# Reading two kinds of PSUM bank at the scheduler's high priority, in a kernel of windowed attention and a feed-forward layer

## The chip, the cores and the metric

The kernel runs on one core of a Trainium2 chip. The metric is the device time of one execution in microseconds (us). Three runs of the kernel before took 719.66, 725.25 and 728.06 us; the median is 725.25 us. One further execution was recorded by the hardware profiler; all views come from it.

Names of engines: PE is TensorE (matmuls), PEld its loading of weights, DVE is VectorE, ACT ScalarE, POOL GpSimd, SP SyncE, whose queue issues most DMAs.

## The reference: what is computed

Attention over q, k, v of shape 4 x 8 x 768 x 64 (batch, heads, positions, head size), where a position sees the last 128 positions and the first 4 ("sinks"), followed by a feed-forward layer on 3072 rows of 512 with a piecewise quadratic activation:

```python
scores = scale * np.matmul(q, k.transpose(0, 1, 3, 2))
keep = is_sink | in_window
a = np.exp(scores - max); a = a / (a.sum() + 1e-9)
x = (a @ v)                      # heads side by side: 3072 x 512
h = x @ w_in                     # 512 -> 2048
g = np.where(h >= 1, h, np.where(h <= -1, 0.0, (h + 1) ** 2 / 4))
out = g @ w_out                  # 2048 -> 512
```

## The kernel before

**Units and waves.** A unit is one batch, one head and half of the positions (3 tiles of 128 rows): 64 units. Eight units, one for each head, make a wave; the attention of a wave runs beside the feed-forward layer of the wave before, so TensorE always has matmuls of both. The first 16 units (the first two waves) take another way, in pairs (`pair_scores`, `early_transp`, `pair_av`). The other 48 are "split" units: each float32 operand is split into a rounded high part and a low remainder, and products are made of the parts. These 48 are what the change touches.

**One split unit, by lines.** `load` brings q and k and splits them (L222 and L225 on ScalarE, L224 on VectorE, L226 on GpSimd). `scores` makes three banks of scores, one for each tile (L240); VectorE reads a bank with the mask and the row maximum (L244), ScalarE takes the exponential (L247), and after the third tile GpSimd and VectorE normalise p (L252, L253, L256, L259) and copy the columns of the sinks to `sk` (L261). `transp`, a unit later, transposes the three tiles of p and `sk` into one bank (L295, L296). That bank is read four times: by ScalarE into the high part of the tiles (L298), by VectorE into their low part (L299), by ScalarE into the high part of the sinks (L300) and by VectorE into their low part (L301). GpSimd then masks the tiles (L304 and L306, each twice) and spreads the sinks (L308). `av`, another unit later, multiplies with v into one bank (L342), which ScalarE (L343) and VectorE (L344, L345) read into the layer's input `xn`. v is split in `values` (L272, L277 on ScalarE, L273, L278 on GpSimd). Tile "r" has one buffer, in which q and v of successive units take turns.

**The feed-forward layer.** `stage1` makes a bank of h (L489); ScalarE and VectorE apply the activation and split the result (L496, L497 on ScalarE, L498 on VectorE, L499 on ScalarE, L500 on VectorE), `stage2` multiplies with the second weights (L508). In 32 units of the later waves `recheck` loads a tile of weights again and takes its top bytes (L196 on ScalarE); in every second of them VectorE folds two such tiles into `both` (L198); L595 to L598 evaluate `both` once, in the last of these.

**What sets the order.** TensorE's order is written out by hand (`attn_steps`, `moe_steps` and `spread`; the pool is entered with `manual_schedule` for TensorE alone). For the other engines the framework's scheduler decides: it plays the program in modelled time and gives an engine, of what is ready, the instruction with the highest priority, which without more is the one that stands first in the program. What it so orders is then fixed: on the chip each engine runs its instructions in that order, and a waiting instruction holds all behind it.

**The banks.** Scores, transposes and p times v share a pool of three banks, `ps_a` (L57). TensorE uses five per unit, in the order scores, scores, scores, transposes, p times v. With three banks that means: the first scores of a unit wait for the last L244 of the unit before, the second scores for L299 and L301 (the bank of transposes), the third for L345 (the bank of p times v), the transposes for the first L244, and p times v for the second L244. Where L345 stands ahead of L301, the second and third scores change places.

Of the kernel before, what the change touches and what calls it, by code (L numbers as in the profile page):

```python
# [8 lines left out]
F32 = mybir.dt.float32  # L9
# [4 lines left out]
ALU = mybir.AluOpType  # L14

B, H, S, D = 4, 8, 768, 64
DM, DFF = 512, 2048
P = 128
# [31 lines left out]
def attn_ffn(ctx, tc, qk, qkp, vx, vs, par, w_in, w_out, out):  # L50
    nc = tc.nc
# [68 lines left out]
    for r0 in (0, 32):  # L120
        r = r0 + CT * NSINK
# [5 lines left out]
    sk1 = const.tile([44, P], F32R, name="sk1")  # L127
# [154 lines left out]
    def transp(u):  # L282
        b, h, t0 = u
        p, sk = st.pop(("p", u))
        T = CT * P
        i0 = int(t0 == 0)
        ns = CT - i0
        r = ns * NSINK
        spt = st["sp", u] = sp[units.index(u) % 2]
        ps = ps_a.tile([P, 512], F32, name="ps_a")  # L290
        pk = ps[:r, T:512]
        pt = st["pt", u] = att.tile([P, 2, CT, 2, P], F32R, name="pt")
        pth, ptl = pt[:, 0], pt[:, 1]
        for i in range(CT):
            nc.tensor.transpose(ps[:, i * P:(i + 1) * P], p[:, i, KB:260], ident)  # L295
        nc.tensor.transpose(pk, sk, ident)  # L296
        full = ps[:, :T].rearrange("p (i q) -> p i q", q=P)
        nc.scalar.copy(pth[:, :, 1], full)  # L298
        nc.vector.tensor_tensor(ptl[:, :, 1], full, pth[:, :, 1].bitcast(F32), op=ALU.subtract)  # L299
        nc.scalar.copy(sk1[0:r], pk)  # L300
        nc.vector.tensor_tensor(sk1[32:32 + r], pk, sk1[0:r].bitcast(F32), op=ALU.subtract)  # L301
        for t in (pth, ptl):
            src = t[:, i0:, 1].bitcast(F32)
            nc.gpsimd.affine_select(out=t[:, i0:, 0], in_=src, pattern=[[0, ns], [-1, P]], base=-1,  # L304
                                    channel_multiplier=1, compare_op=ALU.is_ge, fill=0.0)
            nc.gpsimd.affine_select(out=t[:, i0:, 1], in_=src, pattern=[[0, ns], [1, P]], base=0,  # L306
                                    channel_multiplier=-1, compare_op=ALU.is_ge, fill=0.0)
        nc.gpsimd.tensor_tensor(spt[0:44].rearrange("r (t q) -> r t q", q=P)[:, :ns],  # L308
                                sk1.bitcast(F32).unsqueeze(1).broadcast_to([44, ns, P]),
                                tsel[:, :ns].unsqueeze(2).broadcast_to([44, ns, P]), op=ALU.mult)  # L310

    def av(u):
        b, h, t0 = u
        T = CT * P
        i0 = int(t0 == 0)
        ns = CT - i0
        pt = st.pop(("pt", u))
        spt = st.pop(("sp", u))
        v_s, vs_s = st.pop(("v", u))
        ps = ps_a.tile([P, 512], F32, name="ps_a")  # L320
        r0 = (h % 2) * D
        x = xn[r0:r0 + D, h // 2, :]

        terms = [(2 * CT - 1, 2 * CT)] + [(2 * i + 1, 2 * i + 3) for i in range(CT - 1)] + [None]
        if t0:
            terms.append((0, 1))
        mms = []
        for n, t in enumerate(terms):  # L330
            if t is None:
                w, rhs, c = vs_s, [spt[:, :ns * P]], i0
            else:
                s0, s1 = t
                w, c = v_s[:, (s0 + 1) // 2 - i0], s0 // 2
                rhs = [pt[:, j].rearrange("p i c q -> p (i c q)")[:, s0 * P:s1 * P] for j in range(2)]
                if n == 0:
                    rhs = [pt[:, :, CT - 1, 1]]
            mms += [(w.rearrange("p a d -> p (a d)"), y, c * P) for y in rhs]
        for n, (w, y, c) in enumerate(mms):  # L340
            z = ps[:, c:c + (2 * P if len(y.shape) == 3 else y.shape[-1])]
            nc.tensor.matmul(z, lhsT=w, rhs=y, start=(n == 0), stop=(n == len(mms) - 1))  # L342
        nc.scalar.copy(x, ps[D - r0:P - r0, :T])  # L343
        nc.vector.tensor_tensor(x, ps[r0:r0 + D, :T], x, op=ALU.add)  # L344
        nc.vector.tensor_tensor(x[:, T - P:], ps[r0:r0 + D, T:512], x[:, T - P:], op=ALU.add)  # L345


    def pair_load(m):
# [117 lines left out]
    def attn_steps(n):  # L466
        us = {k: units[n - k] for k in (-1, 0, 1, 2) if 0 <= n - k < len(units)}
        steps = []
        if n == NATIVE:
            steps.append((0.0, lambda: load(us[0])))  # L470
        if -1 in us:
            steps.append((0.0, lambda: load(us[-1])))
        if 1 in us and n - 1 >= NATIVE:
            steps.append((0.0, lambda: values(us[1])))
        steps += [(0.22, lambda i=i: scores(us[0], i)) for i in range(CT) if 0 in us]
        steps += [(0.43, lambda: transp(us[1]))] if 1 in us and n - 1 >= NATIVE else []
        steps += [(1.0, lambda: av(us[2]))] if 2 in us and n - 2 >= NATIVE else []
        if n in CHECK:
            steps.append((0.0, lambda: recheck(n - CHECK[0], n)))
        return steps  # L480
# [119 lines left out]
    ps = ps_a.tile([P, 512], F32, name="ps_a")  # L600
# [56 lines left out]
    with tc.If(other_v > 0):  # L657
        with tc.tile_pool(name="gen", bufs=1) as gen:
# [9 lines left out]
            for t0 in (0, CT):  # L668
                keep = gen.tile([P, CT, S], F32, name="keep")
                kidx = gen.tile([P, S], I32, name="kidx")  # L670
                r = gen.tile([P, S], F32, name="r")
# [55 lines left out]
```

## Time and profile before

| | |
|---|---|
| three runs | 719.66, 725.25, 728.06 us |
| the profiled execution | 724.25 us, of which 722.5 us from first to last instruction |
| mean granted clock of TensorE | 0.991 |
| TensorE busy | 691.1 us, 96% |
| VectorE, ScalarE, GpSimd busy | 530.1, 496.4 and 304.7 us |
| DMA | 73.04 MB, 101 GB/s on average |

The split units run from about 120 to 635 us; after 636 us only the feed-forward layer of the last wave is left. How to read the rows that follow: a row of the timeline has start, length, engine, line, operation, output<-input and, in brackets, the idle time of the engine before it and what ended that. A row of waits has the waiting engine and line, the line waited for, and us in total, times, longest.

Where the text speaks of X, Y and Z, these are three neighbouring units. They recur in each of three waves, those that run near 340, 427 and 514 us, and their instructions stand there in nearly the same order. X is the unit whose rows begin near 427 us in the middle one, Y near 438, Z near 448.

### The profile page before, as it was taken

To read this page: it belongs to the slowest core of one execution; us is meant where nothing else is said; L and a number is where in the kernel's file an instruction comes from. 1 tells how busy PE (TensorE), PEld (TensorE's weight loads), DVE (VectorE), ACT (ScalarE), POOL (GpSimd) and SP (SyncE) were. 2 spreads that over 40 slices of the span, in tenths; PEclk is the share of its full clock that TensorE was granted. 3 is DMA by queue.
4 is the path that set the end of the run, shared out by engine and by line. 5 is a ranking of instruction groups with operands and counts; after the bars stand their busy time and mean duration, and the time that the engine had idled before them with its cause. 6 is when DMAs were issued, how large, how long until landed. Compare 5 with 4: busy or idle time off the path is not lost.

```text
span 722.5 us, 12238 instructions
## 1 busy us (share of the span) xinstructions
PE 691.1 (96%) x3873; PEld 609.8 (84%) x3873; DVE 530.1 (73%) x1345; ACT 496.4 (69%) x1289; POOL 304.7 (42%) x514
## 2 busy tenths in 40 slices
PE   5689999899999999999999999999989999999996
PEld 3467777799899999899889987999979999989895
DVE  8888898978776878788778788878887687733221
ACT  5776777686687877787777777778766867544432
POOL 2003334754452555365555556646556364400000
PEclk9899999999999999999999999999999999999999
DMA  7844333332243434244333443334412220001001
GB/s 230 296 169 166 131 125 96 111 100 57 55 136 97 130 117 124 72 159 126 107 94 86 149 126 115 115 105 140 126 46 69 79 69 17 8 1 44 1 0 49
DMA packets 44840, 73.04 MB, mean 101 GB/s; under 512 B 13024, under 2 KB 29408, under 8 KB 44768
## 3 DMA queue, kind: packets, MB, share of 16 engines
q1 hardware_dynamic: 41504, 59.59, 27.3%
q10 hardware_dynamic: 3264, 12.58, 4.8%
q8 instruction: 33, 0.54, 0.3%
q14 instruction: 39, 0.32, 0.1%
HBM read 65.87 MB, written 6.29 MB: 100 GB/s over the span
## 4 chain that ended last, share of the span: by engine, by line
PE 73%; DVE 15%; ACT 6%; DMA 2%; issue 2%; POOL 1%; SPq 0%; ACTq 0%; DVEq 0%; POOLq 0%
PE o_ps L508 30%; PE h_ps L489 29%; PE ps_a L342 4%; PE ps_a L240 4%; PE ps_a L295 2%; DVE k_s L224 2%; DVE p L259 1%; DVE bits L153 1%; PE ps_a L432 1%; DVE g L498 1%; DMA w<-w_in 1%; DVE gl L500 1%; ACT p L247 1%; DVE p L256 1%; DMA r<-qk 1%
## 5 line engine op out<-in xcount | busy, mean ns | idle before, releaser
L489 PE MATMUL h_ps<-x,wi 128*128 128x384 f32 x1536 | 310.0, 341 | 1.0 <-DVE g L498 1.0
L489 PEld LDWEIGHTS h_ps<-x,wi 128*128 128x128 f32 x1536 | 263.6, 189 | 11.5 <-issue 1.5
L508 PE MATMUL o_ps<-w,gh 128*128 128x512 f32 x768 | 244.4, 399 | 0.0
L508 PE MATMUL o_ps<-w,gl 128*128 128x512 f32 x384 | 151.3, 394 | 0.0
L508 PEld LDWEIGHTS o_ps<-w,gh 128*128 128x128 f32 x768 | 134.3, 189 | 17.7 <-issue 2.8
L496 ACT ACTIVATE g<-h_ps,half 128x384 f32<-128x384 f32 x128 | 73.9, 577 | 59.1 <-PE h_ps L489 58.0
L498 DVE SCALAR_TENSOR_TENSOR g<-g,h_ps 128x384 f32<-128x384 f32 x128 | 70.2, 548 | 57.4 <-ACT g L497 56.4
L226 POOL TENSOR_TENSOR q_l<-r,q_h 128x384 fp32r<-128x384 f32 x48 | 50.4, 1049 | 135.7 <-ACT q_h L225 109.1
L499 ACT CAST gh<-g 128x384 fp32r<-128x384 f32 x128 | 65.5, 512 | 57.6 <-DVE g L498 57.0
L508 PEld LDWEIGHTS o_ps<-w,gl 128*128 128x128 f32 x384 | 72.2, 188 | 17.8
L500 DVE TENSOR_TENSOR gl<-g,gh 128x384 fp32r<-128x384 f32 x112 | 69.0, 616 | 24.4 <-ACT gh L499 23.5
L247 ACT ACTIVATE p<-p,peak 128x260 f32<-128x260 f32 (+1 forms) x144 | 71.4, 496 | 15.8 <-DVE peak L244 15.1
L224 DVE TENSOR_TENSOR k_s<-k_r,k_s 64x524 fp32r<-64x524 f32 (+1 forms) x44 | 47.1, 1070 | 43.3 <-ACT k_s L222 43.2
L244 DVE CUSTOM_DVE_ANT_0 p<-ps_a,m 128x260 f32<-128x260 f32 (+1 forms) x144 | 57.2, 408 | 17.5 <-PE ps_a L240 16.6
L497 ACT ACTIVATE g<-g 128x384 f32<-128x384 f32 x128 | 67.0, 523 | 2.6
L306 POOL TENSOR_SCALAR_AFFINE_SELECT pt<-pt 128x384 fp32r<-128x384 f32 (+1 forms) x96 | 51.3, 534 | 24.0 <-DVE pt L299 21.0
L304 POOL TENSOR_SCALAR_AFFINE_SELECT pt<-pt 128x384 fp32r<-128x384 f32 (+1 forms) x96 | 51.8, 539 | 7.4 <-ACT pt L298 3.1
L259 DVE TENSOR_SCALAR p<-p,stat 128x132 f32<-128x132 f32 (+1 forms) x144 | 54.4, 431 | 0.1
L500 POOL TENSOR_TENSOR gl<-g,gh 128x384 fp32r<-128x384 f32 x16 | 21.9, 1370 | 68.4 <-ACT gh L499 60.5
L342 PEld LDWEIGHTS ps_a<-pt,v_s 128*128 128x128 f32 x304 | 46.4, 188 | 2.2
L342 PE MATMUL ps_a<-pt,v_s 128*128 128x256 f32 (+1 forms) x304 | 46.7, 273 | 0.0
L240 PE MATMUL ps_a<-k_s,q_h 128*128 128x260 f32 (+1 forms) x144 | 40.5, 281 | 5.1 <-DVE sk L301 3.9
(149 smaller groups left out, 1007.7 us busy)
## 6 DMA issues: line engine op xcount, KB each, us to landing
r<-qk SPq DMA_DIRECT2D x48, 192.0 KB
k_r<-qk SPq DMA_DIRECT2D x32, 262.0 KB
again<-w_in SPq DMA_DIRECT2D x16, 512.0 KB
again<-w_out SPq DMA_DIRECT2D x16, 512.0 KB
w<-w_in ACTq DMA_DIRECT2D x6, 1024.0 KB
w<-w_out ACTq DMA_DIRECT2D x6, 1024.0 KB
out<-o SPq DMA_DIRECT2D x23, 256.0 KB
r<-vx SPq DMA_DIRECT2D x32, 128.0 KB
```

Source lines behind the costliest of these rows:

```text
L224: eng.tensor_tensor(k_s[D:P], k_r[D:P], k_s[D:P].bitcast(F32), op=ALU.subtract)
L240: nc.tensor.matmul(ps[:, lo:260], lhsT=q[:, i * P:(i + 1) * P], rhs=k_s[:, c0:c0 + 260 - lo], start=(j == 0), stop=(j == len(qs) - 1))
L247: nc.scalar.activation(p[:, i, lo:260], p[:, i, lo:260], AF.Exp, bias=peak_i, scale=-1.0, accum_out=stat[:, i:i + 1])
L259: nc.vector.tensor_scalar(p[:, i, lo:260], p[:, i, lo:260], stat[:, CT + i:CT + i + 1], None, op0=ALU.mult)
L342: nc.tensor.matmul(z, lhsT=w, rhs=y, start=(n == 0), stop=(n == len(mms) - 1))
L489: nc.tensor.matmul(h_ps[:, :T], lhsT=w_i[j][:, w, ct * P:(ct + 1) * P], rhs=x[:, y, ct], start=(ct == 0 and n == 0), stop=(ct == NCT - 1 a ...
L496: nc.scalar.activation(g, h_ps[:, :T], AF.Relu, bias=half, scale=0.5)
L497: nc.scalar.activation(g, g, AF.Square)
L498: nc.vector.scalar_tensor_tensor(g, g, 1.0, h_ps[:, :T], op0=ALU.min, op1=ALU.max)
L499: nc.scalar.copy(gh, g)
L500: (nc.gpsimd if row0 == GL_POOL else nc.vector).tensor_tensor(gl, g, gh.bitcast(F32), op=ALU.subtract)
L508: nc.tensor.matmul(o_ps[tt], lhsT=gg[:, tt * P:(tt + 1) * P], rhs=w_o[j][:, w], start=(j == 0 and n == 0), stop=(j == NJ - 1 and n == 2))
```

## The change

The four instructions that read a bank of transposes, and the three that read a bank of p times v, are recorded under the scheduler's high priority. Among the first four, the two for the sinks now stand ahead of the two for the tiles.

```diff
-        nc.scalar.copy(pth[:, :, 1], full)
-        nc.vector.tensor_tensor(ptl[:, :, 1], full, pth[:, :, 1].bitcast(F32), op=ALU.subtract)
-        nc.scalar.copy(sk1[0:r], pk)
-        nc.vector.tensor_tensor(sk1[32:32 + r], pk, sk1[0:r].bitcast(F32), op=ALU.subtract)
+
+        with tc.high_priority():
+            nc.scalar.copy(sk1[0:r], pk)
+            nc.scalar.copy(pth[:, :, 1], full)
+            nc.vector.tensor_tensor(sk1[32:32 + r], pk, sk1[0:r].bitcast(F32), op=ALU.subtract)
+            nc.vector.tensor_tensor(ptl[:, :, 1], full, pth[:, :, 1].bitcast(F32), op=ALU.subtract)
...
-        nc.scalar.copy(x, ps[D - r0:P - r0, :T])
-        nc.vector.tensor_tensor(x, ps[r0:r0 + D, :T], x, op=ALU.add)
-        nc.vector.tensor_tensor(x[:, T - P:], ps[r0:r0 + D, T:512], x[:, T - P:], op=ALU.add)
+        with tc.high_priority():
+            nc.scalar.copy(x, ps[D - r0:P - r0, :T])
+            nc.vector.tensor_tensor(x, ps[r0:r0 + D, :T], x, op=ALU.add)
+            nc.vector.tensor_tensor(x[:, T - P:], ps[r0:r0 + D, T:512], x[:, T - P:], op=ALU.add)
```

No instruction is added, dropped or resized, and TensorE's order is the same. In the changed kernel line numbers shift: L300 and L301 (high parts, sinks then tiles), L302 and L303 (low parts) are what were L300, L298, L301 and L299; the masks L304 and L306 become L306 and L308, the sinks' spreading L308 becomes L310, L344 and L345 become L347 and L348, L498 and L500 become L501 and L503. The text names lines by their numbers before, unless it says otherwise.

VectorE in unit X of the wave near 427 us, before (p is the probabilities, pt the transposed ones, sk_133 the sinks' parts, xn the layer's input, g and gl the activation and its low part; ISA with ps_a is the reading of a bank of scores, L244):

```order
L299 TENSOR_TENSOR pt<-ps_a,pt 128x3x128
L259 TENSOR_SCALAR p<-p,stat 128x132 x3
L261 COPY sk<-p 128x12
L344 TENSOR_TENSOR xn<-ps_a,xn 64x384
L301 TENSOR_TENSOR sk_133<-ps_a,sk_133 12x128
L345 TENSOR_TENSOR xn<-ps_a,xn 64x128
L498 SCALAR_TENSOR_TENSOR g<-g,h_ps 128x384
L244 ISA p,peak<-ps_a,m_106 128x260
L244 ISA peak 128x1
L500 TENSOR_TENSOR gl<-g,gh 128x384
L244 ISA p,peak<-ps_a,m_106 128x260
```

The same place in the changed kernel:

```order
L302 TENSOR_TENSOR sk_133<-ps_a,sk_133 12x128
L303 TENSOR_TENSOR pt<-ps_a,pt 128x3x128
L259 TENSOR_SCALAR p<-p,stat 128x132 x3
L261 COPY sk<-p 128x12
L347 TENSOR_TENSOR xn<-ps_a,xn 64x384
L348 TENSOR_TENSOR xn<-ps_a,xn 64x128
L501 SCALAR_TENSOR_TENSOR g<-g,h_ps 128x384
L503 TENSOR_TENSOR gl<-g,gh 128x384
L244 ISA p,peak<-ps_a,m_106 128x260
L244 ISA peak 128x1
L244 ISA p,peak<-ps_a,m_106 128x260
```

The sinks' low part now stands ahead of the tiles'; in this unit, and in X of the two other waves, gl has moved ahead of the first reading of scores as well.

VectorE in unit Y, which follows, before:

```order
L500 TENSOR_TENSOR gl<-g,gh 128x384
L299 TENSOR_TENSOR pt<-ps_a,pt 128x3x128
L259 TENSOR_SCALAR p<-p,stat 128x132 x3
L198 TENSOR_TENSOR both<-both,top 128x256
L261 COPY sk<-p 128x12
L344 TENSOR_TENSOR xn<-ps_a,xn 64x384
L301 TENSOR_TENSOR sk_133<-ps_a,sk_133 12x128
L345 TENSOR_TENSOR xn<-ps_a,xn 64x128
L498 SCALAR_TENSOR_TENSOR g<-g,h_ps 128x384
L500 TENSOR_TENSOR gl<-g,gh 128x384
```

And in the changed kernel:

```order
L302 TENSOR_TENSOR sk_133<-ps_a,sk_133 12x128
L303 TENSOR_TENSOR pt<-ps_a,pt 128x3x128
L259 TENSOR_SCALAR p<-p,stat 128x132 x2
L503 TENSOR_TENSOR gl<-g,gh 128x384
L259 TENSOR_SCALAR p<-p,stat 128x132
L198 TENSOR_TENSOR both<-both,top 128x256
L347 TENSOR_TENSOR xn<-ps_a,xn 64x384
L261 COPY sk<-p 128x12
L348 TENSOR_TENSOR xn<-ps_a,xn 64x128
L501 SCALAR_TENSOR_TENSOR g<-g,h_ps 128x384
```

The sinks' low part has moved six places up, and the first gl from ahead of the tiles' low part to between two of the three normalisations. The second part of xn keeps its place.

GpSimd in unit Y, before (stat is the sum of p, sp_136 the spread sinks, vsx and v_s the low parts of v):

```order
L252 TENSOR_SCALAR stat<-stat 128x3
L304 AFFINE_SELECT pt<-pt 128x3x128
L306 AFFINE_SELECT pt<-pt 128x3x128
L304 AFFINE_SELECT pt<-pt 128x3x128
L278 TENSOR_TENSOR vsx_137<-vs_r,vsx_137 44x64
L273 TENSOR_TENSOR v_s<-r,v_s 128x4x64
L306 AFFINE_SELECT pt<-pt 128x3x128
L308 TENSOR_TENSOR sp_136<-sk_133,tsel 44x384
```

And in the changed kernel:

```order
L252 TENSOR_SCALAR stat<-stat 128x3
L306 AFFINE_SELECT pt<-pt 128x3x128
L310 TENSOR_TENSOR sp_136<-sk_133,tsel 44x384
L308 AFFINE_SELECT pt<-pt 128x3x128
L306 AFFINE_SELECT pt<-pt 128x3x128
L278 TENSOR_TENSOR vsx_137<-vs_r,vsx_137 44x64
L273 TENSOR_TENSOR v_s<-r,v_s 128x4x64
L308 AFFINE_SELECT pt<-pt 128x3x128
```

The spreading of the sinks has moved from the end of the unit's row to its second place among the masks.

Besides these, three output stores move ahead of one load of the sinks' v on SyncE, once in each of three waves, and L596, one of the instructions that evaluate `both`, moves behind L498 in Y of the wave near 514 us.

## The prediction, made before the result was known

> **What bounds the kernel now.** I read the page's busy times first.
>
> ```profile
> span 722.5 us, 12238 instructions
> ...
> PE 691.1 (96%) x3873; PEld 609.8 (84%) x3873; DVE 530.1 (73%) x1345; ACT 496.4 (69%) x1289; POOL 304.7 (42%) x514
> ```
>
> TensorE is busy for 691.1 of 722.5 us. The change touches split units only, so I then took the busy time by stretches, four of them from the part with split units. The columns are start:end, length, and busy us (instructions) of PE, PEld, DVE, ACT and POOL, then clock, DMA share and GB/s.
>
> ```profile
> 216.00:300.00 84.00, 84.00 (x477) 76.66 (x476) 64.85 (x180) 64.94 (x171) 42.12 (x81) 1.00 0.38 116
> 340.00:385.00 45.00, 43.88 (x247) 39.32 (x246) 36.29 (x95) 31.99 (x83) 26.98 (x47) 1.00 0.37 109
> 427.00:470.00 43.00, 40.92 (x234) 36.89 (x233) 35.58 (x94) 31.93 (x83) 26.32 (x46) 1.00 0.38 113
> 514.00:555.00 41.00, 38.93 (x224) 34.97 (x223) 33.79 (x91) 29.03 (x79) 24.59 (x40) 1.00 0.27 74
> ```
>
> From 216 to 300 TensorE has no gap at all: nothing that VectorE or ScalarE does sooner can help there. The other three stretches have 1.12, 2.08 and 2.07 us of gaps, 5.3 us together. The list of TensorE's waits says for what (total us, times, longest):
>
> ```profile
> PE ps_a L240 <- DVE sk L301: 3.9, 5, 1.4
> ...
> PE ps_a L295 <- DVE p L259: 2.3, 1, 2.3
> ...
> PE ps_a L240 <- DVE xn L345: 0.8, 2, 0.4
> ...
> PE ps_a L295 <- DVE peak L244: 0.6, 1, 0.6
> ```
>
> 3.9 us are a scores matmul waiting for a bank of transposes that L301 (the sinks' low part) reads last, 0.8 us one waiting for a bank of p times v (L345), 0.6 us a transpose waiting for a bank of scores (L244). The sum is those 5.3 us. The 2.3 us for L259 are one wait of the first transposes for p itself, before any bank has been read by the lines of the change; no moved instruction feeds it. Here is the largest gap, in unit Y of the wave that begins near 427 us, and its neighbours X (before) and Z (after); start and length in us:
>
> ```profile
> 430.43 0.36 PE L240 MATMUL ps_a<-k_s,q_h 128*128 128x260 f32 x1 [0.28 <-DVE sk L301]
> ...
> 432.38 0.49 PE L295 MATMUL ps_a<-ident,p 128*128 128x128 f32 x3
> ...
> 439.43 0.69 PE L489 MATMUL h_ps<-x,wi 128*128 128x384 f32 x3
> 441.54 0.36 PE L240 MATMUL ps_a<-k_s,q_h 128*128 128x260 f32 x1 [1.42 <-DVE sk L301]
> ...
> 442.89 0.28 PE L240 MATMUL ps_a<-k_s,q_h 128*128 128x260 f32 x1
> ...
> 443.83 0.49 PE L295 MATMUL ps_a<-ident,p 128*128 128x128 f32 x3
> ...
> 451.61 0.36 PE L240 MATMUL ps_a<-k_s,q_h 128*128 128x260 f32 x1 [0.39 <-DVE xn L345]
> ```
>
> The end of a matmul normally lies under the next one. The page's group of L489 has the mean of one:
>
> ```profile
> L489 PE MATMUL h_ps<-x,wi 128*128 128x384 f32 x1536 | 310.0, 341 | 1.0 <-DVE g L498 1.0
> ```
>
> One lasts 0.34 us, three together 0.69 (at 439.43), so they start some 0.17 apart and the last 0.16 or so of each is hidden. A gap then costs its idle time and about 0.16 more: the scores of 441.54 could have begun at 439.43 + 0.53 = 439.96. Eight gaps: 5.3 + 8 x 0.16 = 6.6 us is all that the change can win, 0.9%.
>
> VectorE over X and Y:
>
> ```profile
> 430.32 0.29 DVE L345 TENSOR_TENSOR xn<-ps_a,xn 64x128 f32<-64x128 f32 x1
> 430.64 0.56 DVE L498 SCALAR_TENSOR_TENSOR g<-g,h_ps 128x384 f32<-128x384 f32 x1
> 431.12 0.42 DVE L244 CUSTOM_DVE_ANT_0 p<-ps_a,m 128x260 f32<-128x260 f32 x1
> ...
> 431.78 0.56 DVE L500 TENSOR_TENSOR gl<-g,gh 128x384 fp32r<-128x384 f32 x1 [0.23 <-ACT gh L499]
> 432.25 0.42 DVE L244 CUSTOM_DVE_ANT_0 p<-ps_a,m 128x260 f32<-128x260 f32 x1
> ...
> 434.74 1.09 DVE L224 TENSOR_TENSOR k_s<-k_r,k_s 64x524 fp32r<-64x524 f32 x1 [0.88 <-ACT k_s L222]
> ...
> 437.13 0.54 DVE L299 TENSOR_TENSOR pt<-ps_a,pt 128x384 fp32r<-128x384 f32 x1
> 437.60 1.28 DVE L259 TENSOR_SCALAR p<-p,stat 128x132 f32<-128x132 f32 x3
> 438.80 1.74 DVE L198 TENSOR_TENSOR both<-both,top 128x256 int32<-128x256 int32 x1
> ...
> 441.11 0.28 DVE L301 TENSOR_TENSOR sk<-ps_a,sk 12x128 fp32r<-12x128 f32 x1
> 441.42 0.28 DVE L345 TENSOR_TENSOR xn<-ps_a,xn 64x128 f32<-64x128 f32 x1
> ...
> 442.75 0.56 DVE L500 TENSOR_TENSOR gl<-g,gh 128x384 fp32r<-128x384 f32 x1 [0.58 <-ACT gh L499]
> 443.22 0.42 DVE L244 CUSTOM_DVE_ANT_0 p<-ps_a,m 128x260 f32<-128x260 f32 x1
> ```
>
> L301 ends at 441.39, and TensorE goes on at 441.54. But L345, due for the next scores' bank, ends at 441.70, and L244, due for the transposes' bank, at 443.64. These two stand right behind.
>
> **The change part by part.** *L301 ahead of L299* (L300 ahead of L298 on ScalarE): the transposes' bank is free when L299 ends. In Y that would be 437.67 + 0.31 for the L301 before it, 438.0, against a wish for 439.96: the wait on L301 goes, by 2 us. Nothing is added; the same 0.28 us stand earlier, so the sum up to L345 is the same. L299 and what hangs on it (the masks on GpSimd, p times v a unit later) come 0.3 us later; p times v of that unit stands a whole unit further on in TensorE's order, and the list of waits has none of L342.
>
> *What is late next, if nothing else moved.* Without the wait TensorE wants the next scores at 439.96 + 1.35 (442.89 - 441.54) = 441.3, L345 gives the bank at 441.7; it then wants the transposes 0.94 later at 442.65 and gets the bank at 443.64 + 0.05. The transposes start at 443.7 instead of 443.83. Of 1.58 us freed, 0.1 stays. The rest turns into waits on L345 and L244, which end a row of steps through ScalarE (L498, L499, L500, L244) that the change doesn't shorten.
>
> *L343 to L345.* High priority moves them hardly at all: L345 has the same place among VectorE's instructions in 46 of 48 units. Price zero.
>
> *L500 ahead of the first L244 in X*, at one unit of each of three waves. L500 needs L499, and L499 needs L498, so VectorE now stands still where it did an L244:
>
> ```profile
> 431.23 0.51 ACT L499 CAST gh<-g 128x384 fp32r<-128x384 f32 x1 [1.49 <-DVE g L498]
> 431.65 0.51 ACT L247 ACTIVATE p<-p,peak 128x260 f32<-128x260 f32 x1
> ...
> 434.08 0.62 ACT L222 CAST k_s<-k_r 128x524 fp32r<-128x524 f32 x1
> ```
>
> L500 stays at 431.78, the first L244 goes from 431.12 to 432.25 and ends at about 432.7. The transposes of X, which need its bank, start at 432.75 rather than 432.38: 0.37 later, which eats the 0.44 (0.28 + 0.16) won on 430.43. L247 behind it on ScalarE, 431.65, becomes 432.7, and all behind it up to L222 is late by 1.05: L224 at 435.8. So Y's L345 ends not at 441.7 but at 442.75, the second scores start there (442.89 before), and the transposes 2.0 later (443.69 - 441.70), at 444.7 against 443.83: **+0.9**. Z's wait for L345 ends, since Z's first late bank is the transposes' now: -0.39 - 0.16 = **-0.55**.
>
> *L308 ahead of L306, L304 and L273 on GpSimd.* The row of instructions from which L198 gets no room:
>
> ```profile
> 437.81 0.52 POOL L306 TENSOR_SCALAR_AFFINE_SELECT pt<-pt 128x384 fp32r<-128x384 f32 x1 [1.00 <-DVE pt L299]
> ...
> 439.75 0.51 POOL L306 TENSOR_SCALAR_AFFINE_SELECT pt<-pt 128x384 fp32r<-128x384 f32 x1
> 441.47 0.82 POOL L308 TENSOR_TENSOR sp<-sk,tsel 44x384 fp32r<-44x384 f32 x1 [1.21 <-DVE sk L301]
> ```
> ```profile
> L198 DVE TENSOR_TENSOR both<-both,top x16: 405/656/1742, 208.1 to 524.2; 128x256 int32<-128x256 int32 x16
> ```
>
> L198 lasts 0.41 to 1.74 us (min/median/max ns); here 1.74, ending 0.28 after GpSimd's L306. L308's 0.82 us now lie inside that row, less about 0.45 that fill the time in which GpSimd waited for L299: the row ends some 0.4 later. Against it, L198 itself starts 1.05 later, so less of it is waiting. Bounds for L345 in Y: 1.3 earlier (L198 at its 0.41) to 1.4 later (the second rival). I take 0, between them. [...] L273 frees the tile into which SyncE loads the next q; it ends about 0.4 later, and ScalarE's wait for that load is small in sum:
>
> ```profile
> ACT q_h L225 <- DMA r<-qk: 8.2, 10, 1.8
> ```
>
> None of the ten shows as a gap of TensorE; I price it at 0, at most 0.4 in each of three waves. On SyncE an output store moves ahead of one load of the sinks' v in three places: 0 to 1.8 us each (the longest wait for a load above), taken as 0, since ScalarE comes to that load's cast (L277) only near the unit's end.
>
> *L596 behind L498*, once, in the last wave's Y:
>
> ```profile
> 527.18 0.92 DVE L596 TENSOR_SCALAR both<-both 128x256 int32<-128x256 int32 x1
> ```
>
> It stood ahead of L498, so that row of steps starts **0.9** sooner.
>
> **The sum**, by waves: 340 us, +0.9 - 0.55 = +0.35 (of the two waits for L345, 0.4 each, one is Z's here and one is Z's at 427); 427 us, +0.9 - 0.55 = +0.35 (X even); 514 us, +0.9 - 0.9 - 0.9 = -0.9, where Z's gap is a wait on L301 of about 0.74 ((3.9 - 1.42 - 0.28) / 3) with its 0.16. Together -0.2. The profiled execution took 724.25 us, 1.75 of it outside the span; 724.05 after. The median of the three runs, 725.25, is 1.0 above it. I forecast **724.6**, between the two.
>
> **The rivals.** *The waits simply go* (chance 0.22): scheduling luck in X costs nothing, L198 runs at 0.4, and L345 and L244 come in time. For it: L198 at its shortest frees 1.3 us in each Y. Against it: L244 ends 2 us behind L345 in any case. -6.6 at most, 717.7 to 718.7 by which base is taken; half of it is 721.
>
> *GpSimd's longer row holds VectorE* (0.20), slower than before: L500 now stands between two L259 in Y, where GpSimd works without a pause, and reads two tiles in SBUF as L198 does. If it too waits for the row's end, then L500 0.5, one L259 0.4 and L198 0.4 come after that end, 0.4 later, in place of L198's 0.28: 1.4 later at L345, on top of the sum, in three waves: -0.2 + 4.2 = +4.0, 728.3 to 729.3. It decides once Y's L345 ends more than some 1.1 us after its old 441.70: each 0.1 beyond the 1.05 of the forecast adds 0.1 per wave, and the -0.2 is gone. Against it: L198's median of 0.66 says that most of its sixteen runs are not held for long. [...]
>
> **How the numbers follow.** Forecast (-2 to +2 us) 0.58, waits gone 0.22, GpSimd's row 0.20. The three runs before span 719.66 to 728.06, so a median moves by some 0.3% by itself. Range 719 to 729.5: it leaves out the far end of the first rival and little of the second. 1% is 7.25 us, about what a measurement can tell from no change. Faster by over 1% needs all of the 6.6 us and luck: 0.05. Slower needs the second rival and more: 0.06. Within 1%: 0.89.
>
> **What would show it.** In the profile after: no wait of scores (L240) on the sinks' part; waits on xn's second part (old L345) and, longer, of the transposes on L244, and some 5 us of gaps in the three stretches again; L224 in X about 1 us later relative to TensorE; L198 still long. The forecast is wrong if those stretches have under 2 us of gaps, or if Y's L500 lasts over 1 us.

## The result, and the profile after

The changed kernel takes **751.08 us** (median of 4 runs, 748.42 to 752.95), the kernel before 722.55 us (median of 4 runs, 719.66 to 728.06). The ratio is 1.0363, with a 95% interval of 1.0319 to 1.0408: 3.6% slower. The prediction was 724.6 us, no change, in a range that ended at 729.5.

The page of the changed kernel: the span, the busy times of the engines, and the first line of the chain of waits that ended last.

```profile
span 751.2 us, 12268 instructions
...
PE 701.9 (93%) x3873; PEld 612.8 (82%) x3873; DVE 574.6 (76%) x1345; ACT 492.0 (66%) x1289; POOL 292.1 (39%) x514
...
PE 50%; DVE 31%; ACT 11%; issue 4%; DMA 1%; POOL 1%; ACTq 0%; SPq 0%; DVEq 0%; POOLq 0%
```

VectorE is busy for 44.5 us more (530.1 before) with the same 1345 instructions. Which ones got longer is seen in the groups by line; busy us and mean ns of one stand behind the bar. First the kernel before, with a row of what ScalarE waits for (total us, times, longest):

```profile
L259 DVE TENSOR_SCALAR p<-p,stat 128x132 f32<-128x132 f32 (+1 forms) x144 | 54.4, 431 | 0.1
...
ACT gh L499 <- DVE g L498: 57.0, 73, 3.1
```

and the same rows of the changed kernel, with what TensorE waits for:

```profile
L259 DVE TENSOR_SCALAR p<-p,stat 128x132 f32<-128x132 f32 (+1 forms) x144 | 105.3, 778 | 0.1
...
L198 DVE TENSOR_TENSOR both<-both,top 128x256 int32<-128x256 int32 x16 | 7.0, 436 | 2.3 <-ACT top L196 2.3
...
ACT gh L502 <- DVE g L501: 124.0, 84, 5.0
...
PE ps_a L240 <- DVE xn L348: 11.7, 13, 1.8
...
PE ps_a L295 <- DVE peak L244: 5.0, 9, 0.8
PE o_ps L511 <- DVE gl L503: 4.9, 3, 2.4
```

L259, the three multiplications that normalise p, has gained 50.9 us. L198, the instruction that the prediction watched, lost 6.6 of its 13.6. Everything behind L259 on VectorE is late: ScalarE waits 124.0 us for VectorE's activation where it waited 57.0, and TensorE waits for xn and for the reading of scores.

The stretches of the prediction (busy us of PE, PEld, DVE, ACT, POOL, then clock, DMA share, GB/s):

```profile
340.00:385.00 45.00, 39.50 (x221) 34.63 (x221) 37.13 (x82) 28.20 (x77) 21.79 (x40) 1.00 0.35 102
427.00:470.00 43.00, 39.02 (x218) 34.78 (x218) 36.36 (x83) 26.99 (x72) 20.40 (x39) 0.98 0.35 106
514.00:555.00 41.00, 38.01 (x208) 33.97 (x209) 34.16 (x83) 26.96 (x72) 18.74 (x33) 0.96 0.30 89
```

5.50, 3.98 and 2.99 us of gaps, 12.5 where there were 5.3 (over the same times; the work stands 4 us later than before at the first of them and 21 at the last). Two engines tell why. First VectorE in unit Y of the wave near 427 us, which now runs near 450 (start and length in us):

```profile
450.19 0.28 DVE L302 TENSOR_TENSOR sk<-ps_a,sk 12x128 fp32r<-12x128 f32 x1
450.50 0.56 DVE L303 TENSOR_TENSOR pt<-ps_a,pt 128x384 fp32r<-128x384 f32 x1
450.98 2.89 DVE L259 TENSOR_SCALAR p<-p,stat 128x132 f32<-128x132 f32 x2
453.79 0.55 DVE L503 TENSOR_TENSOR gl<-g,gh 128x384 fp32r<-128x384 f32 x1
454.25 0.28 DVE L259 TENSOR_SCALAR p<-p,stat 128x132 f32<-128x132 f32 x1
```

then GpSimd at the same place:

```profile
449.77 0.68 POOL L306 TENSOR_SCALAR_AFFINE_SELECT pt<-pt 128x384 fp32r<-128x384 f32 x1 [0.20 <-ACT pt L301]
450.56 0.82 POOL L310 TENSOR_TENSOR sp<-sk,tsel 44x384 fp32r<-44x384 f32 x1
451.34 0.51 POOL L308 TENSOR_SCALAR_AFFINE_SELECT pt<-pt 128x384 fp32r<-128x384 f32 x1
451.81 0.51 POOL L306 TENSOR_SCALAR_AFFINE_SELECT pt<-pt 128x384 fp32r<-128x384 f32 x1
452.30 0.31 POOL L278 TENSOR_TENSOR vsx<-vs_r,vsx 44x64 fp32r<-44x64 f32 x1
452.58 0.73 POOL L273 TENSOR_TENSOR v_s<-r,v_s 128x256 fp32r<-128x256 f32 x1
453.27 0.51 POOL L308 TENSOR_SCALAR_AFFINE_SELECT pt<-pt 128x384 fp32r<-128x384 f32 x1
```

One L259 alone takes 0.28 us (454.25). The two before it take 2.89 and end at 453.87, 0.09 after GpSimd's last mask. In the kernel before, GpSimd stood still for 1.00 us until L299 was done, because its second mask overwrites what L299 still reads; its row then began at 437.81, 0.21 after VectorE's first L259 at 437.60, and three L259 took 1.28. Now the spread of the sinks (L310, 450.56) fills that pause, since its input comes from L302, and is under way when VectorE's first L259 arrives at 450.98. So it goes in nearly every unit from 295 us on: 30 of these 31 have an L259 of over 1 us, in the kernel before one of 31.

That GpSimd starts first is not enough, though. In 13 units from 148 to 287 us, where the spread is for two tiles, it is at work too when L259 arrives, mostly for as long, and in 12 of them the first L259 takes its 0.28 us:

```profile
147.98 0.61 POOL L310 TENSOR_TENSOR sp<-sk,tsel 44x256 fp32r<-44x256 f32 x1 [0.22 <-DVE sk L302]
...
148.40 1.06 DVE L259 TENSOR_SCALAR p<-p,stat 128x128 f32<-128x128 f32 x3
```

That spread ends 0.19 us after L259's start (148.59); the longer one of the later units ends 0.40 after it (451.38), with the next masks right behind.

### The profile page after: what moved, and what is told of

Same layout as the page of the kernel before. It is cut to its first block, busy times and chain, and to the rows that moved or that the text cites. A ratio compares the mean times of both kernels' runs of the same rounds, so it can differ in the third digit from the quotient of the medians.

```text
span 751.2 us, 12268 instructions
## 1 busy us (share of the span) xinstructions
PE 701.9 (93%) x3873; PEld 612.8 (82%) x3873; DVE 574.6 (76%) x1345; ACT 492.0 (66%) x1289; POOL 292.1 (39%) x514
## 4 chain that ended last, share of the span: by engine, by line
PE 50%; DVE 31%; ACT 11%; issue 4%; DMA 1%; POOL 1%; ACTq 0%; SPq 0%; DVEq 0%; POOLq 0%
PE o_ps L511 21%; PE h_ps L492 20%; DVE p L259 9%; DVE g L501 2%; ACT p L247 2%; PE ps_a L240 2%; DVE k_s L224 2%; PE ps_a L344 2%; DVE gl L503 2%; DVE pt L303 2%; ACT gh L502 2%; ACT k_s L222 2%; ACT g L499 1%; DVE p L256 1%; DVE bits L153 1%
## 5 line engine op out<-in xcount | busy, mean ns | idle before, releaser
L511 PE MATMUL o_ps<-w,gh 128*128 128x512 f32 x768 | 245.9, 401 | 0.0
L511 PE MATMUL o_ps<-w,gl 128*128 128x512 f32 x384 | 152.7, 398 | 4.9 <-DVE gl L503 4.9
L511 PEld LDWEIGHTS o_ps<-w,gh 128*128 128x128 f32 x768 | 135.4, 190 | 17.7 <-issue 2.8
L502 ACT CAST gh<-g 128x384 fp32r<-128x384 f32 x128 | 65.4, 511 | 124.8 <-DVE g L501 124.0
L501 DVE SCALAR_TENSOR_TENSOR g<-g,h_ps 128x384 f32<-128x384 f32 x128 | 70.3, 549 | 60.8 <-ACT g L500 59.9
L259 DVE TENSOR_SCALAR p<-p,stat 128x132 f32<-128x132 f32 (+1 forms) x144 | 105.3, 778 | 0.1
L511 PEld LDWEIGHTS o_ps<-w,gl 128*128 128x128 f32 x384 | 72.7, 189 | 23.8 <-DVE gl L503 6.2
L503 DVE TENSOR_TENSOR gl<-g,gh 128x384 fp32r<-128x384 f32 x112 | 68.7, 614 | 25.8 <-ACT gh L502 24.8
L224 DVE TENSOR_TENSOR k_s<-k_r,k_s 64x524 fp32r<-64x524 f32 (+1 forms) x44 | 45.7, 1039 | 37.5 <-ACT k_s L222 37.4
L500 ACT ACTIVATE g<-g 128x384 f32<-128x384 f32 x128 | 67.0, 524 | 2.7
L244 DVE CUSTOM_DVE_ANT_0 p<-ps_a,m 128x260 f32<-128x260 f32 (+1 forms) x144 | 55.8, 408 | 6.5 <-PE ps_a L240 5.8
L306 POOL TENSOR_SCALAR_AFFINE_SELECT pt<-pt 128x384 fp32r<-128x384 f32 (+1 forms) x96 | 50.6, 527 | 11.9 <-ACT pt L301 10.0
L240 PE MATMUL ps_a<-k_s,q_h 128*128 128x260 f32 (+1 forms) x144 | 41.5, 288 | 12.1 <-DVE xn L348 11.7
L503 POOL TENSOR_TENSOR gl<-g,gh 128x384 fp32r<-128x384 f32 x16 | 21.8, 1367 | 68.4 <-ACT gh L502 60.5
L344 PEld LDWEIGHTS ps_a<-pt,v_s 128*128 128x128 f32 x304 | 46.4, 188 | 2.3
L308 POOL TENSOR_SCALAR_AFFINE_SELECT pt<-pt 128x384 fp32r<-128x384 f32 (+1 forms) x96 | 47.2, 492 | 1.0
L344 PE MATMUL ps_a<-pt,v_s 128*128 128x256 f32 (+1 forms) x304 | 46.7, 273 | 0.0
```

The source lines that it names most:

```text
L224: eng.tensor_tensor(k_s[D:P], k_r[D:P], k_s[D:P].bitcast(F32), op=ALU.subtract)
L240: nc.tensor.matmul(ps[:, lo:260], lhsT=q[:, i * P:(i + 1) * P], rhs=k_s[:, c0:c0 + 260 - lo], start=(j == 0), stop=(j == len(qs) - 1))
L259: nc.vector.tensor_scalar(p[:, i, lo:260], p[:, i, lo:260], stat[:, CT + i:CT + i + 1], None, op0=ALU.mult)
L500: nc.scalar.activation(g, g, AF.Square)
L501: nc.vector.scalar_tensor_tensor(g, g, 1.0, h_ps[:, :T], op0=ALU.min, op1=ALU.max)
L502: nc.scalar.copy(gh, g)
```

## The experiments

Theory 1, formed on these rows: GpSimd, being at work already, keeps VectorE's L259 out. Theory 2: the new order on VectorE and ScalarE makes a unit's loop longer, and the long L259 is a by-product.

### Is it the priority or the order of the lines?

The changed kernel with the priority taken off L300 to L303, the sinks still written first:

```diff
-        with tc.high_priority():
+        if True:
             nc.scalar.copy(sk1[0:r], pk)
```

> The changed kernel without the scheduler's priority on the four instructions L300 to L303; only the order in which they are written stays, sinks' parts first. PE's order is unchanged, VectorE's differs at a few dozen rows, GpSimd still has the spread before the second mask in nearly every unit. Theory 1: the long L259 stay, time 742 to 753 us. Theory 2, if it is the priority that moves VectorE's and ScalarE's work: back to 718 to 728 us.

750.74 us, ratio 1.0362 (1.0333 to 1.0391): as slow as with the priority.

```profile
L259 DVE TENSOR_SCALAR p<-p,stat 128x132 f32<-128x132 f32 (+1 forms) x144 | 94.4, 704 | 0.2
```

It is the order of the lines. The priority on L345 to L348 changes nothing: without it the changed kernel's instructions stand in the same order, row by row, on TensorE, VectorE, ScalarE and GpSimd.

### Is it the spread's place on GpSimd?

```diff
-            nc.gpsimd.affine_select(out=t[:, i0:, 1], in_=src, pattern=[[0, ns], [1, P]], base=0,
+            mask = nc.gpsimd.affine_select(out=t[:, i0:, 1], in_=src, pattern=[[0, ns], [1, P]], base=0,
...
-        nc.gpsimd.tensor_tensor(spt[0:44].rearrange("r (t q) -> r t q", q=P)[:, :ns],
...
+        with tc.issue_after(mask.ins):
+            nc.gpsimd.tensor_tensor(spt[0:44].rearrange("r (t q) -> r t q", q=P)[:, :ns],
...
```

> The changed kernel with one thing put back: the sinks' spread on GpSimd (L310) is queued behind the unit's last mask, where it stood before the change. VectorE's row differs from the changed kernel's at one place, ScalarE's at a dozen, so the sinks' parts still go ahead of the tiles' there. Theory 1 (the early spread fills the pause of GpSimd, which then keeps VectorE's L259 out over its whole row): L259 comes back from a mean of 778 ns to 400 to 480, its longest instruction from 2.9 us to under 1.6, and the time to 716 to 727 us. Theory 2 (the new order on VectorE and ScalarE makes a unit's loop longer, and the long L259 is a by-product): the time stays at 745 to 753 us, whatever L259 does.

730.51 us, ratio 1.0075 (1.0046 to 1.0104). Putting one GpSimd instruction back, with VectorE's order all but untouched (2 of 1345 rows), takes away four fifths of the loss; as an account of these, theory 2 falls. But 0.75% stays, 3.5 us beyond the expected end, and L259's mean of 491 ns and its longest of 1.62 us are just beyond theirs. VectorE in unit Y of this kernel, behind the row of the group:

```profile
L259 DVE TENSOR_SCALAR p<-p,stat 128x132 f32<-128x132 f32 (+1 forms) x144 | 63.9, 491 | 0.1
...
442.24 0.81 DVE L259 TENSOR_SCALAR p<-p,stat 128x132 f32<-128x132 f32 x2
442.98 0.88 DVE L503 TENSOR_TENSOR gl<-g,gh 128x384 fp32r<-128x384 f32 x1
443.78 1.51 DVE L259 TENSOR_SCALAR p<-p,stat 128x132 f32<-128x132 f32 x1
445.21 1.07 DVE L198 TENSOR_TENSOR both<-both,top 128x256 int32<-128x256 int32 x1
```

L503 now stands between two L259 and lasts 0.88 us, and the L259 and L198 behind it are long too. These are the places of the prediction's second rival, but it is that L259, not L503, which lasts until the unit's last mask has ended (445.29, 0.09 after it). The rival's price was +4.0 us; 0.75% of 724.5 is 5.4 us. How much of that these three units make up, no run shows: L259 of 1.62 us stand near 411 and 500 us as well.

### Is it the form of L259?

Does the hold hang on the form of VectorE's own instruction? L259 in the form that also writes out a sum, put into a column of `stat` that nobody reads any more; in the changed kernel, in the kernel before, and in the changed kernel with the spread last:

```diff
-            nc.vector.tensor_scalar(p[:, i, lo:260], p[:, i, lo:260], stat[:, CT + i:CT + i + 1], None, op0=ALU.mult)
+            nc.vector.tensor_scalar(p[:, i, lo:260], p[:, i, lo:260], stat[:, CT + i:CT + i + 1], None, op0=ALU.mult, op1=ALU.add, accum_out=stat[:, i:i + 1])
```

> The changed kernel with L259 in its form that also writes out a sum over its row (into a column of stat that nobody reads any more); GpSimd's order stays the changed one, spread ahead of the second mask. [...] Theory 2: time stays at 745 to 755.

723.54 us, ratio 0.9981 (0.9963 to 0.9998). GpSimd's order is as in the changed kernel, and against the kernel before the whole loss is gone. Theory 2, with its 745 to 755 us, falls here as well.

```profile
L259 DVE TENSOR_SCALAR_CACHE_REDUCE p<-p,stat 128x132 f32<-128x132 f32 (+1 forms) x144 | 43.2, 343 | 0.1
...
L503 DVE TENSOR_TENSOR gl<-g,gh 128x384 fp32r<-128x384 f32 x112 | 83.1, 742 | 24.4 <-ACT gh L502 23.6
```

> The kernel before with the same form of L259, as the control of the second run. Theory 1: L259 loses its few long instructions (up to 1.55 us), but pays up to 0.3 us more on each of 144, all of it in a VectorE row that has slack in most units: 718 to 727 us. If the sum's own cost is on the path, 724 to 735, and then the second run is read against this one.

719.78 us, ratio 0.9941 (0.9917 to 0.9965). The same form makes the kernel before 0.6% faster: L259 had been held there too, if less. Its rows, the second being the writing out of the sum:

```profile
L259 DVE TENSOR_SCALAR_CACHE_REDUCE p<-p,stat 128x132 f32<-128x132 f32 (+1 forms) x144 | 42.4, 342 | 0.1
...
L259 DVE DVE_READ_ACCUMULATOR p<-p,stat 128x1 f32 x144 | 11.6, 81 | 0.0
```

0.34 + 0.08 us against 0.28 for a free L259: one of this form is longer, but the hold is not seen in it. In the seventh and the tenth run, which have the form too, every row of it between 200 and 665 us lasts 0.33 to 0.35 us. Why this form is not held, no run shows. From the first start to the last end a unit's three take 0.92 us in the mean, where they took 1.15 in the kernel before.

> The changed kernel with both repairs: the spread behind the last mask as in the first run, and L259 in the form with a sum as in the second. Theory 1: nothing of VectorE is held but L503 and L198 at some places; if the new order of VectorE and ScalarE is worth anything by itself, it shows here against the third run (the kernel before with the form with a sum, 719.8 us): 715 to 722 us. Theory 2 in its weak form (the new order costs 4 us by itself, which the second run had over the third): 722 to 726 us.

720.37 us, ratio 0.9953 (0.9932 to 0.9973), against 719.78 for the order before with the same form. With L259's holds out of the way, the new order of VectorE and ScalarE is worth nothing that can be measured, neither way. The second run, with the spread early, lies 0.4% above the third. What is longer there is L503: 742 ns each, where the third run's L500 takes 613 and this run's L503 653. Whether L503, which reads two operands in SBUF, is now the one that is held, and whether the 0.4% are this, is not shown by itself. The third run's kernel and this one are faster than both the kernel before and the changed one.

### More masks on GpSimd

The mask L306 of the rounded part repeated, in the kernel before, once or three times; repeating it changes nothing in the result. The remainder's masks and the spread are queued behind the repeats, to keep their places. The three repeats also with L259 in the form with a sum.

```diff
...
-            nc.gpsimd.affine_select(out=t[:, i0:, 1], in_=src, pattern=[[0, ns], [1, P]], base=0,
-                                    channel_multiplier=-1, compare_op=ALU.is_ge, fill=0.0)
+            for n in range(4 if t is pth else 1):
+                with tc.issue_after(mask.ins) if n else nullcontext():
+                    mask = nc.gpsimd.affine_select(out=t[:, i0:, 1], in_=src, pattern=[[0, ns], [1, P]], base=0,
+                                                   channel_multiplier=-1, compare_op=ALU.is_ge, fill=0.0)
...
```

> The kernel before with GpSimd's second mask (L306) of the rounded part done twice in the same place, which leaves the result as it is: 0.5 us more of GpSimd in each of 46 units, inside the pause of about 1.0 us in which it waits for L299. PE's order is the same as before, ScalarE's differs at some places. Theory 1 (VectorE's L259 is kept out only where GpSimd has no pause left when L259 comes): a pause of 0.5 us is still a pause, L259 stays at a mean of 400 to 500 ns, time 720 to 731 us. Theory 3 (GpSimd's total work counts, whatever the pause): 46 times 0.5 us on the path, 740 to 748 us.

738.57 us, ratio 1.0169 (1.0124 to 1.0214).

> The kernel before with the same mask done four times: 1.5 us more of GpSimd per unit, which fills the pause. PE's order is the same, VectorE's differs at 6 lines and ScalarE's at 18, so no part of the change under study is in it. Theory 1: the pause is gone, L259 is kept out until the row of GpSimd ends, mean of L259 over 700 ns with lengths near 3 us, time 743 to 765 us. Theory 2 (the new order on VectorE and ScalarE is what costs): 720 to 732 us.

729.69 us, ratio 1.0061 (1.0036 to 1.0087).

> The kernel of the sixth run with L259 in the form that also writes out a sum, which the second and third runs showed not to be held. Control of what the longer row of GpSimd costs by itself. Theory 1: no L259 over 0.5 us, what is left is L500 and L198 held (two operands in SBUF), time 718 to 733 us. Theory 3 (GpSimd's longer row costs through the masks that p times v waits for): near the sixth run's time, over 740 us.

725.17 us, ratio 1.0006 (0.998 to 1.0032).

The first two are misses, and their premise was wrong: the pause (1.00 us until 437.81 in Y) stands ahead of this mask, not behind it, so a repeat lengthens the row behind the pause and fills nothing. One repeat costs more than three. With one repeat the scheduler set L278 between the two masks in eight units, and there three L259 took 3.2 to 3.6 us; TensorE's waits show the price:

```profile
PE ps_a L240 <- DVE sk L301: 14.6, 10, 2.2
```

(3.9 in the kernel before). ScalarE's order also differs at 36 rows in that kernel, so its time is not settled by L259 alone. The seventh run is as fast as the kernel before, but its like is the third run, with the same form and the ratio 0.9941: the 1.5 us more of GpSimd per unit cost 0.65% there, about as much as with the plain L259 (0.61%). So they have a price that does not go through L259. L504 lasts 789 ns in the seventh run, its like in the third (L500) 613.

In the changed kernel, the same mask three times. The scheduler puts L278 and L273 between the repeats:

> The changed kernel with GpSimd's second mask of the rounded part (L311 here) done three times, with the same result; the scheduler sets L278 and L273 between the repeats, so that in nearly every unit none of them depends on the one just ahead. VectorE's order differs at 4 lines and ScalarE's at 16, PE's not at all. Theory 1: the unbroken row is 1.0 us longer, and so is L259's time in most of the 30-odd units of the later waves: VectorE 25 to 45 us more in L259, time 765 to 790 us. Rival (GpSimd's instructions let VectorE in one by one, and the length of the row does not matter): 750 to 757 us.

758.89 us, ratio 1.0481 (1.0443 to 1.0519). A miss:

```profile
L259 DVE TENSOR_SCALAR p<-p,stat 128x132 f32<-128x132 f32 (+1 forms) x144 | 106.5, 786 | 0.1
```

GpSimd is busy for 347.3 us instead of 292.1, its row is 1.0 us longer, and L259 has gained 1.2 us in sum. So the sum of the holds does not follow the number of GpSimd's instructions. The time is 1.2% above the changed kernel's all the same, and no run shows through what.

Last, the work on v queued behind the last mask, for which `values` is also called later, behind `scores` and `transp`:

```diff
+        with tc.issue_after(st["mask"]):
+            nc.gpsimd.tensor_tensor(v_s[:, :, j, :], v_r, v_s[:, :, i, :].bitcast(F32), op=ALU.subtract)
...
+        st["mask"] = mask.ins
...
```

> The changed kernel with GpSimd's work on v (L273, L278) queued behind the unit's last mask, and the last two masks therefore next to each other, the second depending on the first. GpSimd's row per unit is then mask, spread, mask, mask, mask, v, v; ScalarE's and VectorE's orders move in many places too, since the copies of v come later. Theory 1: VectorE gets in between the last two masks, 1.3 us after its arrival, with one or two of its three L259; mean of L259 500 to 700 ns against 778, time 733 to 747 us. If only the row's total length counts: L259 as long as in the changed kernel, 748 to 755 us.

750.1 us, ratio 1.0352 (1.0296 to 1.0409). L259 came down as expected, the time did not:

```profile
L259 DVE TENSOR_SCALAR p<-p,stat 128x132 f32<-128x132 f32 (+1 forms) x144 | 76.7, 581 | 0.4
...
L507 DVE SCALAR_TENSOR_TENSOR g<-g,h_ps 128x384 f32<-128x384 f32 x128 | 70.2, 548 | 90.2 <-ACT g L506 89.0
```

With the copies of v later, ScalarE's and VectorE's orders moved in many places, and VectorE waits 89.0 us for ScalarE's L506 (59.9 for the same line in the changed kernel). Too much moved to read the time as L259's: inconclusive.

### One instruction at a time

Three kernels carry small trials behind the last output tile of the kernel before: a row on GpSimd, started by a signal from VectorE, and one instruction of VectorE sent into it.

> The kernel before with a row of small trials behind its last output tile, on tables that nobody reads any more; its total time says nothing. In each trial GpSimd gets N masks of 128x256 in a row (N is 0, 1, 2, 4, 8), VectorE does two multiplications with a sum written out, about 1 us, and then one instruction of 128x132: a multiplication by a scalar as L259 (one operand), a maximum of two operands in SBUF, or a multiplication with a sum. Two more trials have 8 memsets for the masks. Theory 1: the one-operand instruction lasts 0.3 us at N of 0 and 1 and until the end of the whole row at 4 and 8, so several masks long and not just the one that ran when it came; the form with the sum lasts 0.34 us at any N. [...]

Beside eight masks, each working on the tile of the one ahead of it, 3.73 us in all:

```profile
718.54 0.29 DVE L626 TENSOR_SCALAR m<-m,half 128x132 f32<-128x132 f32 x1
```

Not held in sight; beside eight memsets on one place it lasts 0.41 us. So theory 1's "until the end of the row" fell in this form, and a second version was tried: a row of masks that do not depend on each other.

> The kernel before with trials behind its last output tile, as in the eighth run; the total time says nothing. Now GpSimd's N masks write N different places and none depends on the one ahead of it; one trial keeps the in-place chain of the eighth run. The instruction tested on VectorE is one of 128x132, sent about 1 us after the row's start. Theory 1 as the traces of the kernels now have it (VectorE is kept out over a run of GpSimd instructions that do not depend on the one just ahead, and gets in where one does or where GpSimd pauses): beside 8 independent masks the multiplication by a scalar lasts until the row's end, 2 to 3 us; beside the chain of 8 at most 0.5 us; two operands in SBUF beside 8 independent masks also 2 to 3 us; the form with a sum 0.35 us. Rival (each GpSimd instruction lets VectorE in at its end, and the long L259 of the kernels have another cause): at most 0.8 us beside either row. The eighth run gave 0.29 us beside the chain of 8, where both say the same.

Beside eight independent masks, beside the chain of eight, and beside a copy with seven memsets (one operand, then two; the last row is GpSimd's seven memsets of the one-operand trial):

```profile
719.27 0.42 DVE L631 TENSOR_SCALAR p<-m,half 128x132 f32<-128x132 f32 x1
...
722.70 0.29 DVE L631 TENSOR_SCALAR p<-m,half 128x132 f32<-128x132 f32 x1
...
733.86 1.46 DVE L631 TENSOR_SCALAR p<-m,half 128x132 f32<-128x132 f32 x1
...
736.41 0.30 DVE L633 TENSOR_TENSOR p<-m,m1n 128x132 f32<-128x132 f32 x1
```
```profile
733.41 1.82 POOL L617 MEMSET pt<- 128x256 f32 x7
```

Beside the independent masks, eight in 2.91 us from 718.48 on, the instruction lasts 0.42 us, 0.13 longer than beside the chain, and ends at 719.69, 1.70 before their row; that second version fell too. Beside the seven memsets the one-operand instruction lasts until their row has ended, at 735.23. The instruction with two operands in SBUF took 0.30 us beside the memsets.

> The kernel before with trials behind its last output tile; the total time says nothing. GpSimd gets rows of six instructions in the kernel's own shapes, each writing its own place: six masks of 128x384, six subtractions of 128x256, six spreads of 44x384, six memsets, and twice the split unit's mixed row (spread, mask, mask, small subtraction, subtraction, mask, and the same with the small subtraction left out and the last two changed round). VectorE sends one multiplication by a scalar of 128x132 about 0.6 us after the row's start; on the mixed row also three of them, one with two operands in SBUF, and one with a sum. Theory A (what the operation of GpSimd is decides whether VectorE gets in at its end: the ninth run let it in beside masks of 128x256 after one or two, beside memsets only at the row's end): the pure rows come out differently, the memsets held to the end, and one of masks, subtractions or spreads is held to the end too, 1.5 us or more. Theory B (the mixed row's cadence does it, none of its operations by itself): the four pure rows but the memsets let VectorE in within 0.9 us, the mixed row holds it for 1.5 us or more. Theory C (the kernel's own signals between engines do it): every row but the memsets lets it in within 0.9 us.

VectorE's instruction beside six masks, six subtractions, six spreads, and the mixed row of the split units; then two operands and the form with a sum on the mixed row:

```profile
716.73 0.55 DVE L649 TENSOR_SCALAR p<-p,half 128x132 f32<-128x132 f32 x1
722.41 0.68 DVE L649 TENSOR_SCALAR p<-p,half 128x132 f32<-128x132 f32 x1
...
729.32 0.84 DVE L649 TENSOR_SCALAR p<-p,half 128x132 f32<-128x132 f32 x1
...
741.10 1.80 DVE L649 TENSOR_SCALAR p<-p,half 128x132 f32<-128x132 f32 x1
...
759.68 1.75 DVE L645 TENSOR_TENSOR p<-m,p 128x132 f32<-128x132 f32 x1
...
765.72 0.35 DVE L647 TENSOR_SCALAR_CACHE_REDUCE p<-p,half 128x132 f32<-128x132 f32 x1
```

GpSimd's mixed row in the trial of 741.10, up to where VectorE got in:

```profile
741.04 0.82 POOL L621 TENSOR_TENSOR pt<-sk,tsel 44x384 fp32r<-44x384 f32 x1 [2.71 <-DVE pt L633]
741.82 0.99 POOL L618 TENSOR_SCALAR_AFFINE_SELECT pt<-pt 128x384 fp32r<-128x384 f32 x2
742.78 0.31 POOL L626 TENSOR_TENSOR pt<-m,m1n 44x64 fp32r<-44x64 f32 x1
```

Theory B holds but for the memsets (0.81 us beside six of them, 1.66 us long, not to their end). Beside a row of one kind the instruction waits for about the one that runs (0.55, 0.68, 0.84 us for masks, subtractions and spreads of 0.5, 0.7 and 0.8 us); in the mixed row, with no other work about, it waits for the spread and both masks and ends at 742.90, 0.09 after the second mask (741.82 + 0.99). In a second trial, with the row's later part changed, it lasts 1.79 us. This kind of row is thus enough for a hold, without the rest of the kernel. Why a mixed row does it and a pure one does not, no run shows; that stays open.

What VectorE runs counts too: the form with a sum took 0.35 us on the mixed row, and two operands in SBUF took 1.75 us there against 0.30 beside the memsets. VectorE stayed out over three of GpSimd's instructions in the trial (1.80 us from 741.10), and over most of a row in the changed kernel (2.89 us from 450.98, two L259).

## Why the prediction was wrong, step by step

**L308 ahead of L306, L304 and L273 on GpSimd: the step that failed.** It was right that the spread fills the time in which GpSimd waited for L299 ("less about 0.45 that fill the time"), and counted that as a saving. Without the pause of 1.00 us two L259 took 2.89 us, where three had taken 1.28. L259 reads one operand, and the step took only L198 and L500, with two operands, as open to a hold; so its bounds for L345 in Y, 1.3 earlier to 1.4 later, did not contain L259's 2.89 us. There was a sign: three L259 in 1.28 us at 437.60, when one alone takes 0.28, and the group's mean of 431 ns. L198's 1.74 us were another: no GpSimd instruction beside it lasts longer than 0.73 us, so a hold could already be seen to outlast one instruction. And the step looked at three Y units, where the hold is in 30 of the 31 units from 295 us on. 50.9 us more of L259 became 28.5 us of time.

**The second rival** named the right kind of mechanism, GpSimd's row holding VectorE, with 0.20. Instruction, places and size were off: +4.0 us in three units where the kernel lost 28.5. Something near it appears in the run with the spread last, whose whole loss is 5.4 us. Its price was worked out for L500 alone; the rows of L259 beside GpSimd's row, in the same trace, were left out of it.

**L301 ahead of L299**: right. No scores wait for the sinks' part, and **what is late next** is as told, the second part of xn (11.7 us) and the reading of scores (5.0 us), only far longer. The transposes' waits were to be the longer ones, and are the shorter.

**L343 to L345, price zero**: right; without that edit the order is the same on the four engines. **L500 ahead of the first L244, L596, and the sum of -0.2 us**: not to be seen in the changed kernel, but the tenth run against the third sets the two orders beside each other without L259's holds: 720.37 against 719.78 us, no difference that can be measured. The first rival, that the waits simply go and 6.6 us with them, has no support there either.

**What would show it**: three signs were right (no wait for the sinks' part, waits on xn, waits of the transposes). L224 in X stands 5.57 us behind X's second scores (443.21 to 448.78) where it stood 4.31 behind (430.43 to 434.74), near the 1 us that was forecast. "L198 still long" was wrong, a mean of 436 ns for 851. "Some 5 us of gaps again" was 12.5. The sign that was to prove the forecast wrong, L500 over 1 us in Y, did not come (0.55 us): it stood on the wrong instruction.

**TensorE's own part** was in no step. Its idle time went from 31.4 to 49.3 us, and its busy time from 691.1 to 701.9, with the same matmuls. Half of the latter is clock. In slices of 2 us (length, busy us, clock, DMA share, GB/s):

```profile
418.00:420.00 2.00, 0.55 (x3) 1.00 0.06 24
420.00:422.00 2.00, 1.08 (x4) 0.68 0.32 78
422.00:424.00 2.00, 2.00 (x7) 0.50 0.11 34
```

TensorE waits 2.38 us for L503 until 420.92, and from 420.71 on its granted clock is half, for 3.41 us. It is the same with gaps of 1.81 us (until 468.19) and 1.85 us (until 515.16). In slices of 10 us from 300 to 660, four show 0.83, 0.92, 0.90 and 0.83; what they lack, 1.7 + 0.8 + 1.0 + 1.7, is 5.2 us. In the kernel before no such slice is below 0.99.

## What to carry to other kernels

Before an instruction is moved on GpSimd, look at what VectorE does beside it, one-operand multiplications included, and at who is still at work when the other arrives: a pause on GpSimd that looks like waste may be worth keeping (here it was 1.00 us in a unit, and the kernel that filled it has 50.9 us more of L259). In these profiles the hold shows as a busy VectorE instruction that is several times its own shortest (2.89 us for two, where one takes 0.28) and ends just after a GpSimd instruction (0.09). Writing out an unused sum made each L259 0.14 us longer by its rows and took the hold away (a mean of 342 ns in the kernel before); it was worth 0.6% in a kernel that nobody suspected of holds.

## What the runs showed of the hardware that was not expected

A VectorE instruction of 0.28 us was kept out over several GpSimd instructions in succession, 1.80 us in a trial with nothing else running, while a row of six equal masks held it for 0.55 us. Seven memsets, which read nothing, held the one-operand multiplication to their end (1.46 us) and did not touch the one with two operands (0.30 us); but six memsets in another trial held the former for 0.81 us only, before their end, and no run shows why.

TensorE's granted clock was 0.50 for 3.41 us at three places of the changed kernel: from 420.71 us on, 0.21 before the end of the gap of 2.38 us, and from 468.49 and 516.28 on, 0.30 and 1.12 after the ends of those of 1.81 and 1.85. By the slices above some 5.2 us are missing there, on top of the waits themselves. The length of the gap alone doesn't decide it: after a fourth gap of 1.81 us in the same kernel (until 373.44) the clock was 1.00 up to 410, and after one of 2.07 us in the kernel without the priority (until 337.64) two L511 took 0.62 us, where two took 1.05 at the half clock (421.95). What decides it, no run shows.
